# A list scheduler is replaced by one written-out order of all operations

## The chip, the cores and the metric

The kernel runs on one core of one Trainium2 chip. The metric is the device time of one execution in microseconds (us). Inputs and outputs are bf16.

## The reference

Two layers are computed on the same weights, each an attention block and a gated feed-forward block (FFN), for 2048 tokens of 512 features. The attention has 32 heads of 16 features and works on 4 segments of 512 tokens: inside a segment it is causal softmax attention, and a memory matrix `M` and a vector `z` carry the earlier segments.

```python
for s in range(N):                       # N = 4 segments of L = 512 tokens
    logits = einsum('bhqd,bhkd->bhqk', qs, ks) * scale + mask
    a_dot = softmax(logits) @ vs
    pq = phi(qs)                         # t + 1 where t > 0, else exp(t)
    a_mem = (pq @ M) / (pq @ z + 1e-06)
    o = g * a_mem + (1 - g) * a_dot      # g = sigmoid(beta)
    M, z = M + phi(ks).T @ vs, z + sum(phi(ks))
...
x = x + A(layernorm(x)); x = x + B(layernorm(x))   # B: (silu(x@w1) * (x@w3)) @ w2
x = x + A(layernorm(x)); x = x + B(layernorm(x))   # the second layer, same weights
```

## The kernel before

The work is cut into eight stages, numbered 0 to 7: four segments of layer one, then four of layer two. `build` adds 3629 operations to a `Sched` object, stage by stage. An operation is one instruction or a small fixed group of them (a score block is eight matmuls or four), with what it reads and writes and the engines that may run it. `add` numbers them in the order in which they are added (`seq`). Names that the text uses, written name/stage:

- `xt`, `xT`: normalised x turned over, on TensorE or by a DMA transpose on SP's queue; `q`, `k`, `v`: projections, four matmuls to a tile; `evq`, `evk`, `evv`, `evX`: copies of a PSUM bank to SBUF, which ScalarE or VectorE may run (`ev`).
- `R0.0` to `R0.19`: the score blocks of a stage (`attention`; stage 0 is done in two halves and has 40). Each fills all of the PSUM space for scores (two slots `S` of two banks), and one `exp` on ScalarE empties it, so a score block waits for the exp of the one before. GpSimd then cuts the causal corner (`mask`, an affine_select).
- `C0.0` to `C3.0`: exp times values; then `evX`, a DMA transpose `XT`, the division (`rd`, `rdg`, `t2`, `oadd` on VectorE or GpSimd), a DMA transpose `oT`, and the output projection `o0` to `o3`.
- `phexp`, `ph1`, `phmin`: phi; `dacc`, `mden`, `mnum`: the memory's update and reading; `lnve`, `lnrs`, `norm`, `bnst`, `bnag`: layer norm.
- `r`, `g`, `u`, `d`: the FFN's matmuls, eleven to a tile for `d`, four for `g` and `u`; `tanh`, `gp`, `hm`: its gating on ScalarE and VectorE.

PSUM is cut into two slots `S` for scores and four banks `B` that all other matmuls share. TensorE has three ways of working: whole array (F), four row groups (R, the score blocks), four column groups (C, the products with values). `shape` looks at what stands between two score blocks: where a C operation is among them and all others can be cut, these are issued as four quarter matmuls (`quarters`, L393) instead of one whole (`whole`, L388).

The order on each engine comes from `schedule`, a list scheduler: it keeps modelled times, offers each engine its ready operations and takes one by priority, margins and look-ahead (`PRIO`, `GATE`, `FINE`, `MARGIN`, `SLACK`, `LOOK`). The order is fixed when the program is built; on the chip each engine runs its list from front to back, and waits on semaphores where an operand, a buffer or a bank isn't ready. `hand_over` then adds dependencies that the data doesn't need: an instruction of GpSimd waits for the VectorE instructions of certain kinds (`SHARED`) that stand ahead of it, if its modelled start is less than 2 us behind theirs. `finalize` turns dependencies into waits.

Of the kernel before, what the change touches and what calls it, by code (L numbers as in the profile page):

```python
# [9 lines left out]
T = 2048  # L10
# [15 lines left out]
DMA_K = 8  # L26
LAT = 80.0
LAT_SAME = 30.0
DMA_SLACK = 1200.0
LOAD_RATE = 280.0  # L30
PE_SWITCH = 100.0
PE_TAIL = 170.0
R_SLACK = 0.0
SLACK = {"pe": 37.0, "act": 72.0, "dve": 89.0, "pool": 112.0, "sp": 27.0}
LOOK = {"pe": 91.0, "act": 30.0, "dve": 20.0, "pool": 80.0, "sp": 302.0}
C_AGE = 6933.0
MARGIN = {"": 50.0, "XT": 1200.0, "bnag": 500.0, "bnst": 100.0, "d": 200.0, "dacc": 300.0, "evX": 100.0, "evk": 500.0, "evq": 100.0, "evv": 300.0, "exp": 50.0, "g": 50.0, "gpr": 200.0, "hT": 100.0, "hmr": 500.0, "k": 50.0, "ldbeta": 500.0, "ldw": 500.0, "ldwk": 50.0, "ldwo": 3000.0, "ldwq": 300.0, "ldwv": 800.0, "ldx": 50.0, "lnrs": 800.0, "lnve": 300.0, "macc": 50.0, "mask": 50.0, "mblk": 500.0, "mde": 200.0, "mden": 200.0, "mnum": 500.0, "mrec": 1200.0, "norm": 300.0, "oT": 3000.0, "oadd": 500.0, "om": 50.0, "ph": 500.0, "phexp": 200.0, "phmin": 300.0, "pkT": 3000.0, "q": 200.0, "r": 300.0, "resA": 100.0, "resB": 500.0, "stx": 300.0, "t": 2000.0, "tanh": 50.0, "u": 50.0, "warm": 100.0, "xT": 800.0, "xt": 200.0}
# [23 lines left out]
class Op:  # L61
    __slots__ = ("opts", "eng", "fn", "dmaq", "deps", "gates", "prio", "mode", "bufs", "nblock", "succ", "seq",
                 "issued", "start", "end", "lane", "val", "vc", "waits", "name", "size", "avail_at", "hold", "group", "wide", "flex")


class Sched:
# [16 lines left out]
    def add(self, opts, fn, reads=(), writes=(), bufs=(), prio=0.0, mode=None, dmaq=None, name="", gates=(), size=0,  # L83
            hold=(), after=(), flex=False):

        op = Op()
        op.opts = {e: (o, l) for e, o, l in opts}
        op.fn, op.dmaq, op.prio, op.mode, op.name, op.size = fn, dmaq, prio, mode, name, size
        op.bufs = tuple(bufs)
        op.hold = tuple(hold)  # L90
        op.issued = False
        op.avail_at = 0.0
        op.end = 1e12
        op.eng = None
        op.wide = None
# [3 lines left out]
        deps = {}  # L99
# [17 lines left out]
        op.gates = [g for g in gates if g is not None]  # L117
# [6 lines left out]
    @staticmethod  # L124
    def _lat(d, e):
        if d.dmaq is not None:
            return LAT + (DMA_SLACK if e in ("pe", "dve") else 0.0)
        return LAT_SAME if d.eng == e else LAT

    def settle(self, unit_ops, prio, gate, fine):  # L130

        order = list(unit_ops)
        place = {u: i for i, u in enumerate(order)}
        seen = {}
        for op in self.ops:
            key = (op.name, op.group[1])
            seen[key] = seen.get(key, -1) + 1
            op.prio += prio.get(op.group, 0.0) + fine.get(key + (seen[key],), 0.0)
            out = []
            for x in op.gates:  # L140
                if not isinstance(x, tuple):
                    out.append(x)
                elif x in place:
                    i = place[x] + gate.get(op.group, 0)
                    if i >= 0:
                        out.append(unit_ops[order[min(i, len(order) - 1)]])
            op.gates = out

    def schedule(self):
        avail = {e: [] for e in ENGS}  # L150
        for op in self.ops:
            op.succ = []
            op.nblock = 0
        for op in self.ops:
            for d in list(op.deps.values()) + op.gates:
                d.succ.append(op)
                op.nblock += 1
        for op in self.ops:
            if op.nblock == 0:
                for e in op.opts:  # L160
                    avail[e].append(op)
        t_free = {e: 0.0 for e in ENGS}
        busy = {e: 0.0 for e in ENGS}
        dma_free = 0.0
        xpose_free = {}
        pe_mode = "F"
        dma_count = {}
        dma_hist = {}
        order = {e: [] for e in ENGS}
        issue = []  # L170
        left = len(self.ops)
        count = {e: 0 for e in ENGS}
        while left:
            best = None
            for e in ENGS:
                tf = t_free[e]
                cands = []
                smin = None
                for op in avail[e]:
                    s = op.avail_at if op.gates else 0.0  # L180
                    for d in op.deps.values():
                        if e == "pe" and d.eng == "pe" and d.dmaq is None:
                            continue
                        r = d.end + self._lat(d, e)
                        if r > s:
                            s = r
                    ok = True
                    for b in op.bufs:
                        if b.slot is None:
                            if not b.pool.free:  # L190
                                ok = False
                                break
                            r = min(self._slot_ready(b.pool, i, e) for i in b.pool.free)
                        else:
                            r = self._prev_ready(b.prev, e)
                        if r > s:
                            s = r
                    need = {}
                    for b in op.hold + op.bufs:
                        if b.slot is None:  # L200
                            need[b.pool.name] = need.get(b.pool.name, 0) + 1
                            if need[b.pool.name] > len(b.pool.free):
                                ok = False
                    if not ok:
                        continue
                    w = max(tf, s + (R_SLACK if op.mode == "R" else SLACK[e]) + MARGIN.get(op.group[0], 0.0))
                    s = max(tf, s)
                    cands.append((s, w, op))
                    if smin is None or w < smin:
                        smin = w  # L210
                if not cands:
                    continue
                lim = max(smin, tf) + LOOK[e]
                pick = None
                for s, w, op in cands:
                    if w > lim:
                        continue
                    pr = op.prio
                    if e == "pe" and op.mode == "C":
                        if pe_mode == "F" and s - op.avail_at < C_AGE:  # L220
                            pr = 1e5 + pr
                        else:
                            pr = -1e5 + pr
                    if pick is None or (pr, s, op.seq) < pick[0]:
                        pick = ((pr, s, op.seq), s, op)
                s, op = pick[1], pick[2]
                if best is None or s < best[0]:
                    best = (s, e, op)
            if best is None:
                raise RuntimeError("stuck: " + "; ".join(  # L230
                    "%s %s" % (op.name, [b.pool.name for b in op.bufs + op.hold if b.slot is None]) for e in ENGS for op in avail[e][:4]))
            s, e, op = best
            if e == "pe" and op.mode != pe_mode:
                s += PE_SWITCH
                pe_mode = op.mode
            for x in op.opts:
                avail[x].remove(op)
            op.eng = e
            op.issued = True
            op.start = s  # L240
            occ, lat = op.opts[e]
            for b in op.hold + op.bufs:
                if b.slot is None:
                    i = min(b.pool.free, key=lambda i: (self._slot_ready(b.pool, i, e), i))
                    b.pool.free.remove(i)
                    b.slot = i
                    b.prev = b.pool.prev[i]
            for b in op.bufs:
                for d in b.prev:
                    if d is not op:  # L250
                        op.deps[d.seq] = d
                b.left -= 1
                if b.left == 0:
                    b.pool.free.append(b.slot)
                    b.pool.prev[b.slot] = b.users
            if op.dmaq is None:
                op.end = s + lat
                t_free[e] = s + occ
                count[e] += 1
                op.lane = self._lane(("eng", e))  # L260
                op.val = count[e]
            else:
                if op.mode == "T":
# [3 lines left out]
                    if dma_free > x0:  # L267
                        dma_free += 500.0
# [958 lines left out]
```

## Time and profile before

| | |
|---|---|
| time, median of 3 runs | 481.24 us (481.15 to 481.86) |
| span of the profiled execution | 480.1 us |
| what lies around the span, median less span | 1.2 us |
| TensorE busy | 470.7 us, 98% of the span |
| ScalarE, VectorE, GpSimd busy | 390.3, 388.1, 242.6 us |

The span is that of the profiled execution, from its first instruction to its last. Matmuls are pipelined and their ends are modelled: two of them that follow each other overlap in the rows, so the busy time of TensorE counts as busy some time in which it could have begun another matmul.

### The profile page before, as it was taken

Reading aid. Unit: us, or ns where it says so; the run is one execution under the profiler, and the core shown is the slowest. Engines: PE = TensorE matmul, PEld = TensorE weight load, DVE = VectorE, ACT = ScalarE, POOL = GpSimd, SP = SyncE. Lnnn points to the kernel's source line nnn. Section 1 sums busy time; section 2 is a strip of 40 time slices with the busy share of each in tenths; the row PEclk is TensorE's granted clock in tenths of the full one; section 3 lists DMA queues with packets and bytes.
Section 4 is the critical chain, followed back from the end, with each engine's and each line's share of the span. In section 5 each row is a group of like instructions: output and inputs, shape, how many; then the busy total and the mean of one; then the engine's idle time right before and its main releaser. Section 6 shows DMA issues by size and latency. Waiting matters only on the chain.

```text
span 480.1 us, 14316 instructions
## 1 busy us (share of the span) xinstructions
PE 470.7 (98%) x6122; PEld 221.4 (46%) x6122; DVE 388.1 (81%) x816; ACT 390.3 (81%) x351; POOL 242.6 (51%) x383
## 2 busy tenths in 40 slices
PE   8999999999999999999999999999999999999997
PEld 4443446754444344434444444544444344454544
DVE  6988889896988879979987699785985696478672
ACT  3999999988899898899989999889889898930220
POOL 4867484854477545555555355445567456530000
PEclk9999999999999999999999999999999999999999
DMA  8794654423156421471552425431137224320301
GB/s 258 269 155 96 102 123 89 66 52 69 23 89 100 68 35 32 80 110 25 84 84 56 78 46 108 60 59 29 35 45 114 64 29 83 67 47 25 90 3 45
DMA packets 106527, 37.15 MB, mean 77 GB/s; under 512 B 99200, under 2 KB 104448, under 8 KB 106464
## 3 DMA queue, kind: packets, MB, share of 16 engines
q1 hardware_dynamic: 104016, 31.41, 34.7%
q0 software_dynamic: 1488, 4.03, 3.9%
q8 instruction: 48, 0.79, 0.7%
q10 hardware_dynamic: 960, 0.79, 0.5%
q14 instruction: 15, 0.12, 0.1%
HBM read 8.43 MB, written 2.10 MB: 22 GB/s over the span
## 4 chain that ended last, share of the span: by engine, by line
PE 79%; ACT 12%; DMA 3%; DVE 3%; POOL 1%; issue 0%; ACTq 0%; POOLq 0%; DVEq 0%
PE psall L388 45%; PE psall L393 19%; ACT e L958 10%; PE psall L949 9%; PE psall L1000 6%; ACT px L807 1%; DMA xg<-xs 1%; DMA x_tok<-in_A_x_dram 1%; DMA W<-og 1%; DMA W<-xn 1%; POOL e L971 1%; PE psall L834 0%; POOL og L1033 0%; DVE ln L687 0%; DVE W L811 0%
## 5 line engine op out<-in xcount | busy, mean ns | idle before, releaser
L958 ACT ACTIVATE e<-psall 128x2048 bf16<-128x2048 f32 (+1 forms) x180 | 301.5, 1722 | 31.8 <-PE psall L949 30.6
L971 POOL TENSOR_SCALAR_AFFINE_SELECT e<-e 128x512 bf16<-128x512 bf16 x256 | 160.8, 646 | 166.0 <-ACT e L958 115.4
L388 PE MATMUL psall<-W,w 128*128 128x512 bf16 (+1 forms) x494 | 103.4, 351 | 0.5 <-DVE W L546 0.3
L388 PEld LDWEIGHTS psall<-W,w 128*128 128x128 bf16 x494 | 44.8, 98 | 43.5 <-issue 7.7
L1117 DVE SCALAR_TENSOR_TENSOR gp<-th,psall 128x512 bf16<-128x512 bf16 x80 | 53.6, 678 | 12.2 <-ACT th L1115 11.6
L1115 ACT ACTIVATE th<-psall 128x512 bf16<-128x512 f32 x80 | 47.1, 600 | 18.2 <-PE psall L393 17.3
L1121 DVE SCALAR_TENSOR_TENSOR h<-gp,psall 128x512 bf16<-128x512 bf16 x80 | 53.9, 680 | 9.8 <-PE psall L388 8.7
L388 PE MATMUL psall<-w,h 128*128 128x512 bf16 (+1 forms) x216 | 51.9, 380 | 0.0
L393 PE MATMUL psall<-W,w 128*32 128x512 bf16 (+1 forms) x904 | 49.9, 368 | 0.0
L687 DVE BATCH_NORM_STATS2 ln<-x_tok 128x6 f32<-128x512 bf16 x64 | 42.4, 678 | 1.5 <-DMA x_tok<-in_A_x_dram 1.2
L949 PE MATMUL psall<-W 16*128 16x256 bf16 (+3 forms) x544 | 41.7, 294 | 1.0 <-ACT e L958 1.0
L1000 PE MATMUL psall<-e,va 128*32 128x256 bf16 (+3 forms) x1088 | 41.4, 293 | 0.4 <-POOL e L971 0.3
L949 PE MATMUL psall<-W,km 32*128 32x256 bf16 (+3 forms) x544 | 41.1, 291 | 0.4 <-ACT e L958 0.2
L1140 DVE TENSOR_TENSOR x_tok<-psall,x_tok 128x512 bf16<-128x512 f32 (+1 forms) x33 | 22.0, 668 | 21.4 <-PE psall L388 12.3
L546 DVE CAST W<-psall 128x512 bf16<-128x512 f32 x46 | 31.2, 681 | 5.5 <-PE psall L388 5.5
L546 DVE CAST xs<-psall 128x512 bf16<-128x512 f32 x38 | 25.6, 680 | 11.4 <-PE psall L1000 11.3
L949 PEld LDWEIGHTS psall<-W 16*128 16x128 bf16 x544 | 13.2, 91 | 44.9 <-ACT e L958 41.1
L1000 PEld LDWEIGHTS psall<-e,va 128*32 128x32 bf16 x1088 | 24.2, 96 | 18.7 <-POOL e L971 3.1
L393 PEld LDWEIGHTS psall<-W,w 128*32 128x32 bf16 x904 | 23.2, 97 | 20.5 <-issue 0.9
L388 PE MATMUL psall<-W,wk 128*128 128x512 bf16 (+1 forms) x131 | 31.9, 354 | 0.7 <-DVE W L546 0.5
L393 PE MATMUL psall<-w,h 128*32 128x512 bf16 (+3 forms) x588 | 32.0, 363 | 0.0
L1033 POOL TENSOR_TENSOR og<-xg,rd 128x256 bf16<-128x256 bf16 (+1 forms) x46 | 26.0, 581 | 10.4 <-DVE rd L1027 7.3
(85 smaller groups left out, 591.8 us busy)
## 6 DMA issues: line engine op xcount, KB each, us to landing
w<-in_B_w_dram SPq DMA_DIRECT2D x4, 688.0 KB, 8.5
out_dram<-x_tok SPq DMA_DIRECT2D x15, 128.0 KB, 1.7
km<-W POOLq DMA_DIRECT2D x24, 64.0 KB, 2.9
w<-in_B_w_dram POOLq DMA_DIRECT2D x3, 384.0 KB, 3.7
x_tok<-in_A_x_dram POOLq DMA_DIRECT2D x2, 512.0 KB, 4.9
xg<-xs SPq DMA_TRANSPOSE x36, 3.2
W<-og SPq DMA_TRANSPOSE x36, 2.5
wk<-in_A_wk_dram SPq DMA_DIRECT2D x1, 512.0 KB, 4.8
```

The source lines that it names most:

```text
L388: return e.matmul(out, lhsT, rhs, **k)
L393: o = e.matmul(out[c:c + 32], lhsT[:, c:c + 32], rhs, tile_position=(0, c), **k)
L546: return e.tensor_copy(dst(), src())
L687: dve(lambda e: e.bn_stats(ln_r[st.slot][:, i, 0:6], x_tok[:, tt, :]), 540, reads=[("x", tt)], writes=[(st, 0, i)], bufs=[st], prio=prio, ...
L949: o = e.matmul(S4[:, sps(pg), c:c + n], kk[32 * pg:32 * pg + r, G, 128 * j:128 * j + 128], q_r[z.q.slot][32 * pg:32 * pg + r, G, 128 * t1 ...
L958: act(lambda e, N=N, ebuf=ebuf, pgs=pgs, sps=sps: e.activation(e_r[ebuf.slot][:, pgs[0]:pgs[-1] + 1, 0:N], S4[:, sps(pgs[0]):sps(pgs[-1]) ...
L971: pool(lambda e, ebuf=ebuf, c=c: e.affine_select(e_r[ebuf.slot][:, :, c:c + 128], e_r[ebuf.slot][:, :, c:c + 128], pattern=[[0, 4], [1, 128]],
L1000: o = e.matmul(bank(X)[32 * pg:32 * pg + 32, base + W - n:base + W], va_r[z.va.slot][:, j, h:h + 32], e_r[eb.slot][:, pg, c:c + n], start= ...
L1033: return e.tensor_tensor(ogv()[:, 0:nt, :, k, :], src, v(1)[:, k, :, :, None].to_broadcast([P, nt, 4, DH]), ALU.mult)
L1115: act(lambda e, NW=NW, B=B, th=th: e.activation(th_r[th.slot][:, 0:NW], bank(B)[:, 0:NW], ACT.Tanh, scale=0.5), NW, reads=[(B, 0)], writes ...
L1117: dve(lambda e, NW=NW, B=B, th=th, gp=gp: e.scalar_tensor_tensor(gp_r[gp.slot][:, 0:NW], th_r[th.slot][:, 0:NW], 1.0, bank(B)[:, 0:NW], AL ...
L1121: dve(lambda e, NW=NW, B=B, gp=gps[fg], h=hs[fg]: e.scalar_tensor_tensor(h_r[h.slot][:, 0:NW], gp_r[gp.slot][:, 0:NW], 0.5, bank(B)[:, 0:N ...
```

## The change

`schedule` no longer schedules. It reads the order of all 3629 operations from a list of their numbers (`ORDER`), and takes the second of an operation's two possible engines for the 188 numbers in `OTHER`. The list is one for all engines; each engine takes its own out of it in that order. Buffer slots are handed out first in, first out. All priorities, margins, gates and cost parameters are gone. In place of `hand_over` each GpSimd instruction that isn't a DMA waits for all `SHARED` operations of VectorE that stand between it and the GpSimd instruction ahead of it, however far back they are.

```diff
     def schedule(self):
-        avail = {e: [] for e in ENGS}
...
+        self.issue = []
+        for run in ORDER.split():
+            a, _, b = run.partition("-")
+            self.issue += self.ops[int(a):int(b or a) + 1]
+        other = {int(x) for x in OTHER.split()}
+        self.order = {e: [] for e in ENGS}
...
+        for place, op in enumerate(self.issue):
+            e = op.eng = op.opts[1 if op.seq in other else 0]
+            op.place = place
             for b in op.hold + op.bufs:
                 if b.slot is None:
-                    i = min(b.pool.free, key=lambda i: (self._slot_ready(b.pool, i, e), i))
...
+                    b.slot = b.pool.free.pop(0)
+                    b.prev = b.pool.prev[b.slot]
...
+            if e == "dve" and op.group[0] in SHARED:
+                handed.append(op)
+            elif e == "pool" and op.dmaq is None:
+                for d in handed:
+                    op.deps[d.seq] = d
+                handed = []
+            self.order[e].append(op)
...
-    def hand_over(self):
-
-        place = {op.seq: n for n, op in enumerate(self.issue)}
-        todo = [op for op in self.order["pool"] if op.dmaq is None]
-        for d in self.order["dve"]:
-            if d.group[0] not in SHARED or d.start > HAND_OVER:
-                continue
-            while todo and place[todo[0].seq] < place[d.seq]:
-                todo.pop(0)
-            if todo and todo[0].start < d.start + 2000.0:
-                todo[0].deps[d.seq] = d
...
-            need = sorted((d for d in bylane.values() if kn[d.lane] < d.val), key=lambda d: -d.end)
+            need = sorted((d for d in bylane.values() if kn[d.lane] < d.val), key=lambda d: -d.place)
...
+ORDER = """
+    24 8 1 23 26 25 28 27 29 4 0 16 9 2 5 3 18 10 6-7 11 17 19 12 22 20-21 32 13-14 30 15 33 31 34 42 35 55 54 36
...
+    1124 1102-1105 770 747 774 771 1289 333-335 1162 1125 336 375 374 748 1290 743 1293 1116 744 784 776 785 1137
+    1117-1118 377 1136 378-380 382-385 775 1291 381 386 376 772 745 769 788 746 1119 869 396 870 1120 387 1138 397
...
+    1223-1224 643 1593 1590 644 1539-1542 628-630 1226 1543 910 631-632 1227 1533 633 645 1230 1594 1208 1210 1240
...
+    1000-1004 1969 1264 1970-1971 1950 1612 1951 1972 1282 1611 1958 1610 2114 1613 1959 2115-2116 1615 1614
+    1960-1961 1987-1990 1616 1982-1983 1962 1952 1617 1984-1985 989-992 1992 1619 1993-1994 993 1991 1995 1986 1266
...
+    3421 3410 3422 3416 3423-3424 3411 3425 3185-3190 3141-3144 3191 3426 3431 3427 3433 3429 3428 3434 3432 3430
+    3435 3192 3145 3136-3140 3172-3182 3159-3169 3436-3439 3441 3440 3442 3193-3194 3183 3195-3197 3184 3146-3154
+    3443 3155-3156 3444 3448 3157-3158 3449-3450 3445 3170 3446-3447 3451-3452 3454-3457 3460-3463 3453 3488-3489
...
-    S.settle(units, PRIO, GATE, FINE)
```

What the numbers in these lines are: 377 to 380 are `o2`/0, 382 to 385 `o3`/0, 770, 784 and 788 the score blocks `R0.6`, `R0.7`, `R0.8` of stage 1; 1226 and 1240 are `R0.11` and `R0.12` of stage 2, 631 and 632 two matmuls of `d2`/0, 1230 `C1.0`/2, 1594 `mden`/3; 1612 and 1616 are `R0.2` and `R0.3` of stage 3, 1951, 1958 to 1961 and 1987 to 1990 the nine matmuls between them, 2114 a `phexp`, 1613 the exp behind it; 3425 is the last matmul of `o3`/7, 3185 to 3195 are `d3`/6, 3172 to 3182 `d2`/6, 3159 to 3169 `d1`/6, 3146 to 3156 `d0`/6, 3141 to 3144 `u9`/6, 3136 to 3139 `u8`/6, 3443, 3444 and 3448 `r0`, `r1` and `r2` of stage 7, whose input two `xT` transposes bring (3439 and 3442).

## Rows read from the trace of the kernel before

**Rows 1.** The page's first part: busy time, share of the span, instructions of each engine.
```profile
span 480.1 us, 14316 instructions
...
PE 470.7 (98%) x6122; PEld 221.4 (46%) x6122; DVE 388.1 (81%) x816; ACT 390.3 (81%) x351; POOL 242.6 (51%) x383
```

**Rows 2.** Busy us by stretch: its length, PE, PEld, DVE, ACT, POOL, clock, DMA.
```profile
0.00:11.00 11.00, 8.75 (x62) 4.79 (x64) 6.97 (x21) 3.07 (x4) 5.82 (x17) 1.00 0.78 246
11.00:62.00 51.00, 50.60 (x722) 22.41 (x711) 45.79 (x113) 50.75 (x56) 33.02 (x54) 1.00 0.69 159
62.00:118.00 56.00, 54.22 (x860) 32.50 (x861) 48.17 (x104) 52.30 (x47) 34.01 (x53) 1.00 0.44 79
118.00:420.00 302.00, 300.89 (x3372) 132.51 (x3374) 248.66 (x510) 272.15 (x226) 164.57 (x253) 1.00 0.38 64
420.00:449.00 29.00, 28.67 (x564) 14.38 (x560) 21.35 (x41) 5.69 (x11) 5.14 (x7) 1.00 0.25 57
449.00:477.00 28.00, 27.58 (x572) 14.86 (x572) 17.14 (x29) 6.30 (x11) 0.00 (x0) 1.00 0.09 26
```

**Rows 3.** TensorE's timeline around seven holes: start, us, instruction, idle before, its releaser.
```profile
69.60 0.83 PE L393 MATMUL psall<-wo,W 128*32 128x512 bf16 x12 [0.60 <-DMA W<-og]
...
76.42 0.83 PE L388 MATMUL psall<-W,w 128*128 128x256 bf16 x6 [0.35 <-DVE W L546]
...
81.35 0.40 PE L949 MATMUL psall<-W 16*128 16x512 bf16 x4 [0.26 <-ACT e L958]
...
86.24 0.29 PE L949 MATMUL psall<-W 16*128 16x256 bf16 x4 [0.18 <-ACT e L958]
...
137.58 0.29 PE L949 MATMUL psall<-W 16*128 16x256 bf16 x4 [0.55 <-ACT e L958]
...
157.52 0.82 PE L388 MATMUL psall<-W,wk 128*128 128x512 bf16 x3 [0.22 <-DVE gp L1117]
...
438.81 9.04 PE L393 MATMUL psall<-w,h 128*32 128x512 bf16 x164
...
448.93 0.27 PE L393 MATMUL psall<-w,W 128*32 128x192 bf16 x4 [0.33 <-DMA W<-xn]
```

**Rows 4.** TensorE's timeline, one run of whole matmuls between two score blocks.
```profile
218.30 0.39 PE L949 MATMUL psall<-W,km 32*128 32x512 bf16 x4
...
219.28 1.89 PE L388 MATMUL psall<-wv,W 128*128 128x512 bf16 x8
221.10 0.40 PE L949 MATMUL psall<-W,km 32*128 32x384 bf16 x8
```

**Rows 5.** ScalarE's timeline over the same run.
```profile
217.93 1.05 ACT L807 ACTIVATE px<-W 128x1024 bf16<-128x1024 bf16 x1
218.87 1.87 ACT L958 ACTIVATE e<-psall 128x2048 bf16<-128x2048 f32 x1
```

**Rows 6.** ScalarE's groups by form: busy us, mean ns, idle before and its releasers.
```profile
L958 ACT ACTIVATE e<-psall 128x2048 bf16<-128x2048 f32 x140 | 263.6, 1883 | 31.1 <-PE psall L949 30.0
...
L807 ACT ACTIVATE px<-W 128x1024 bf16<-128x1024 bf16 x24 | 26.7, 1111 | 0.3 <-DVE W L546 0.2
L545 ACT ACTIVATE xs<-psall 128x512 bf16<-128x512 f32 x26 | 15.8, 608 | 1.5 <-PE psall L1000 1.5
```

**Rows 7.** Waits, engine and line, for whom: us in total, times, longest.
```profile
POOL e L971 <- ACT e L958: 115.4, 90, 3.7
...
POOL e L971 <- DVE xn L705: 14.2, 14, 2.4
...
PEld psall L1000 <- POOL e L971: 3.1, 8, 0.7
```

**Rows 8.** A VectorE line by itself: duration ns min/median/max.
```profile
L705 DVE TENSOR_SCALAR xn<-x_tok,ln x64: 318/406/787, 6.2 to 444.7; 128x512 bf16<-128x512 bf16 x64
```

**Rows 9.** Another VectorE line, with a PSUM operand: duration ns min/median/max.
```profile
L1121 DVE SCALAR_TENSOR_TENSOR h<-gp,psall x80: 620/681/689, 81.2 to 467.2; 128x512 bf16<-128x512 bf16 x80
```

**Rows 10.** Waits of SP's DMA queue: us in total, times, longest.
```profile
SPq L1041 <- POOL e L971: 48.8, 14, 10.0
```

More of the change, by code (lines that the diff above doesn't have):

```diff
@@ L26 @@
 DMA_K = 8
[L27 to L31, printed above, removed]
-PE_TAIL = 170.0
[L33 to L37, printed above, removed]
+PE_TAIL = 170.0
 class Pool:
@@ L61 @@
 class Op:
-    __slots__ = ("opts", "eng", "fn", "dmaq", "deps", "gates", "prio", "mode", "bufs", "nblock", "succ", "seq",
-                 "issued", "start", "end", "lane", "val", "vc", "waits", "name", "size", "avail_at", "hold", "group", "wide", "flex")
+    __slots__ = ("opts", "eng", "fn", "dmaq", "deps", "mode", "bufs", "hold", "seq", "place", "lane", "val", "vc", "waits", "name",
+                 "group", "wide", "flex", "gates")
 class Sched:
@@ L86, in add @@
         op = Op()
-        op.opts = {e: (o, l) for e, o, l in opts}
-        op.fn, op.dmaq, op.prio, op.mode, op.name, op.size = fn, dmaq, prio, mode, name, size
+        op.opts = [e for e, _, _ in opts]
+        op.fn, op.dmaq, op.mode, op.name = fn, dmaq, mode, name
         op.bufs = tuple(bufs)
         op.hold = tuple(hold)
-        op.issued = False
-        op.avail_at = 0.0
-        op.end = 1e12
         op.eng = None
+        op.gates = []
         op.wide = None
@@ L116, in add @@
         op.deps = deps
-        op.gates = [g for g in gates if g is not None]
         for b in op.bufs:
@@ L122, in add @@
         return op
[L124 to L147, printed above, removed]
@@ L149, in schedule @@
-    def schedule(self):
-        avail = {e: [] for e in ENGS}
[L151 to L171, printed above, removed]
-        count = {e: 0 for e in ENGS}
[L173 to L182, printed above, removed]
-                            continue
[L184 to L241, printed above, removed]
@@ new lines, in schedule @@
+    def schedule(self):
+        self.issue = []
[4 more added lines that the diff above has]
+        self.order = {e: [] for e in ENGS}
+        count = {e: 0 for e in ENGS}
+        sent = {}
+        handed = []
+        for place, op in enumerate(self.issue):
+            e = op.eng = op.opts[1 if op.seq in other else 0]
+            op.place = place
@@ L284, in schedule @@
-            busy[e] += occ
-            order[e].append(op)
-            issue.append(op)
-            left -= 1
-            for nx in op.succ:
-                nx.nblock -= 1
-                if nx.nblock == 0:
-                    nx.avail_at = s
-                    for x in nx.opts:
-                        avail[x].append(nx)
-        self.order, self.issue, self.busy = order, issue, busy
-        self.hand_over()
+                op.lane, op.val = self._lane(("eng", e)), count[e]
+            else:
+                q = sent.setdefault(op.dmaq, [])
+                n = len(q)
+                op.lane, op.val = self._lane(("dma", op.dmaq, n % DMA_K)), 16 * (n // DMA_K + 1)
+                if n >= DMA_K:
+                    op.deps[q[n - DMA_K].seq] = q[n - DMA_K]
+                q.append(op)
@@ L296, in schedule @@
+            if e == "dve" and op.group[0] in SHARED:
[3 more added lines that the diff above has]
+                    op.deps[d.seq] = d
+                handed = []
+            self.order[e].append(op)
+        assert sorted(op.seq for op in self.issue) == list(range(len(self.ops)))
+        for op in self.issue:
+            assert all(d.place < op.place for d in op.deps.values())
         self.shape()
-        self.t_total = max(op.end for op in self.ops)
@@ L397 @@
 SHARED = ("norm", "lnve", "t", "rdg", "ph", "phmin", "mblk", "km", "oadd")
-HAND_OVER = 1e9
 def o_act(n, psum=True):
@@ L454, in build @@
+"""
+OTHER = """
[8 rows of a table added]
+"""
 def build(nc, A_x, A_wq, A_wk, A_wv, A_wo, A_beta, B_w1, B_w3, B_w2, out):
```

180 lines of the change are left out of this document (121 added, 59 removed), and 19 rows, old and new, of tables (FINE, OTHER).

## The prediction

> **What bounds the kernel now.** The page comes first: TensorE is busy for 470.7 of 480.1 us, ScalarE and VectorE for 81% each [rows 1]. So the order can only win what TensorE idles, and the next view is where it does. By stretches [rows 2] it idles 2.25 us in the first 11 us (loads and the first layer norm), 0.40 from 11 to 62, 1.78 from 62 to 118, 1.11 from 118 to 420, 0.33 from 420 to 449 and 0.42 behind that; about 3 us more lie behind its last matmul. Between 11 and 449 us that is 3.62 us, and the change is mostly about them.
>
> The timeline shows them as separate holes. Seven stand in [rows 3], with 2.49 of the 3.62 us; the reader is to see that they have different releasers: a DMA transpose twice, ScalarE's exp three times, VectorE twice. A hole is longer than the idle time shown. Eight whole matmuls fill 1.89 us and each is drawn 0.38 us long [rows 4], so one begins every (1.89 - 0.38) / 7 = 0.216 us, and each is drawn 0.16 us past the point where the next could begin. I add 0.16 us to each hole.
>
> The last view is the beat of the attention. A score block waits for the exp ahead of it. A run of eleven matmuls lasts 2.80 us from score block to score block (218.30 to 221.10) [rows 4], of which 11 x 0.216 = 2.38 are the matmuls and 0.42 the score block and two changes of mode. So a run of n matmuls lasts 0.42 + 0.216 n: nine make 2.37 us. ScalarE needs 1.88 for the exp and whatever stands ahead of it: 1.11 for a `phexp`, 0.61 for a bank copy [rows 6]. TensorE is the bound by a little; where the order gives ScalarE too much in one run, or TensorE too little, a hole appears.
>
> **The change part by part.** *The same work.* The list holds the same 3629 operations. Counted from both orders, TensorE changes its mode 357 times in place of 358, and 497 operations are cut into quarters in place of 490. A change of mode is about 0.1 us (eight matmuls from 219.28 would let the next begin at 221.01, the score block begins at 221.10 [rows 4]), and a quartered operation streams as fast as a whole one: 164 quarters, 41 operations, take 9.04 us, 0.22 each [rows 3]. Together: -0.1 us.
>
> *Four holes that the list fills.* At 69.60, `o2`/0 waits for the transpose of `og`; it stood ahead of score block `R0.6`. Now it stands behind `R0.7` (784, then 377), one run and two score blocks later, at least 2.4 us by the beat, against a hole of 0.60. At 137.58 the run ahead of `R0.12` of stage 2 held `C1.0` and one `mnum`, too little for the exp; now it holds two matmuls of `d2`/0, `C1.0` and `mden`, so the two alone add 0.43 and the rest at least nothing, against 0.55. At 448.93, `r2`/7 waits for the transpose of the layer norm; between the last `o`/7 and the `r`s stood 41 operations [rows 3]. In the new list 50 stand ahead of `r0`, and two more ahead of `r2`: 11 x 0.216 = 2.4 us more cover, against 0.33. At 86.24 the run of stage 1 that held `C1.0`, `dacc` and three `u` now holds eight `u` ahead of `C1.0` and three behind it, half-size matmuls of about 0.11: +0.9 less `dacc`, against 0.18. Sum: 0.60 + 0.55 + 0.33 + 0.18 + 4 x 0.16 = 2.3 us. What moves into these runs leaves others; it is late there only if that run falls under the exp's need, which is the part after next.
>
> *The other holes.* The three left in [rows 3] (0.35, 0.26, 0.22) and those not shown (3.62 - 2.49 = 1.13) make 1.96 us, with 0.16 for each of the three 2.4. The list rewrites their surroundings (1026 of 1931 neighbouring pairs on TensorE stay), but I see no single move that closes them. Ends: 0 and 2.4; I take half, 1.2, since nothing in the rows favours either end.
>
> *New pressure on ScalarE.* Six bank copies leave it (0.61 each, 3.6 us of 390). But the list puts short runs beside long ScalarE work. Between `R0.2` and `R0.3` of stage 3 (1612 to 1616) stand nine matmuls, 2.37 us, and a `phexp` with an exp, 1.11 + 1.88 = 2.99: short by 0.62. Counted like this over stages 2 to 7, eleven runs fall short by more than 0.45 us, 6.5 us together (the longest 0.79); the old order had two such. A shortage isn't all lost. In [rows 4, 5] eleven matmuls, 2.80, stand against the same 2.99, short by 0.19, yet there is no hole: the `phexp` began 0.37 us ahead of the score block, and the exp ended at 220.74, 0.36 us ahead of the next. So ScalarE may be short by 0.19 + 0.36 = 0.55 when it comes early. By that row the eleven cost 0.7 us in all; if ScalarE isn't early, 6.5. I take 1.1, near the end that a row shows.
>
> *VectorE and its queue.* It gains six copies at about 0.68 (as [rows 9], also with a PSUM operand) and loses one `t2`: 388.1 becomes about 392 of 480. What hides this is TensorE's runs; without cover each copy holds one of the four banks 0.68 us longer, as the holes of 76.42 and 157.52 show (0.35 and 0.22). Nothing is added for it.
>
> *The hand-over to GpSimd.* Counted from both orders, 215 VectorE operations are handed over in place of 191, to 97 GpSimd instructions in place of 131. A wait there holds the masks queued behind it, and those hold a C operation. GpSimd is busy for half the span [rows 1], already waits 14.2 us for `norm` alone, and TensorE waits for masks 3.1 us [rows 7]. Ends: -3.1 and +3.1; I take 0, since the masks mostly wait for the exp (115.4 us) and their consumers stand two score blocks later.
>
> The trace shows the reason for such waits: `norm`, with all operands in SBUF, takes from 318 to 787 ns with a median of 406 [rows 8], while an instruction with a PSUM operand stays between 620 and 689 [rows 9]. The Trainium skill (GPSIMD Engine Reference, section 1, Specifications) says that GpSimd shares its SBUF interfaces with VectorE, with contention when VectorE runs in a 2-port mode or with two SBUF inputs; the spread agrees, though no row here isolates it. By that rule VectorE would come earlier wherever the new waits keep the two apart, which is the first rival below; by the rows alone the term stays 0.
>
> *SP's queue, start and end.* The transposes on SP go in a new order, and its queue stands behind waits for masks for 48.8 us [rows 10]; a transpose in the wrong place would make a hole like the one at 69.60, 0.8 us. I take 0, with one such as bound. The first score block still has the same projections ahead of it, and the last piece is still half a tile of `d3`: 0.
>
> **The sum.** -0.1 - 2.3 - 1.2 + 1.1 = -2.5 us. The profiled execution: span 480.1, to 477.6; with the 1.2 us that lie around it, against the median of 481.24, **478.7 us**.
>
> **The rivals.**
> 1. *All holes close.* VectorE comes earlier because the port is free, the 2.4 us of other holes go wholly, and ScalarE's shortage costs nothing: -0.1 - 2.3 - 2.4 = -4.8, 476.4 us. For it: two of the holes end with VectorE. Against it: one list for all engines can't please every run.
> 2. *No change.* TensorE's work is the same, and each hole closed is paid by another of its size, since work moved into one run leaves another: 481.2 us. For it: TensorE is at 98%. Against it: three of the four closed holes are late data, which a move cures without cost.
> 3. *ScalarE becomes the bound in the attention* (the other side). At the eleven short runs it isn't early, so each costs its full shortage: -3.6 + 6.5 = +2.9, 484.1 us. It decides from 3.6 us on, a third of a microsecond for each. For it: several come close to each other, so that one exp's delay passes to the next; [rows 5] has only one. Against it: six copies less on ScalarE.
>
> **How the numbers follow.** Forecast (476.8 to 480.2 us, from just above rival 1 to a gain that can just be told) 0.55; rival 1 (below 476.8), 0.13; rival 2, 0.14; rival 3 and, in part, a transpose issued late, 0.18. A measurement of this kernel tells about 0.2%, 0.96 us, from no change. Faster by more: 0.55 + 0.13 = 0.68; within: 0.14; slower: 0.18. The range of 475.4 to 482.9 leaves out 0.07 below (the hand-over's gain on top of rival 1) and 0.12 above, most of rival 3.
>
> **What would show it.** Right: idle of TensorE from 11 to 449 us falls from 3.62 to about 2, the holes at `o2`/0, ahead of `R0.12` of stage 2 and at `r2`/7 are gone, and those left end with ScalarE. Rival 3 would show as holes of 0.3 us and more ahead of score blocks in stages 2 to 6, with an exp as their releaser; rival 1 as less than 1 us idle and a median of `norm` near its 318 ns. Wrong: a C operation that waits for GpSimd in every stage, or an `o` or `r` behind a transpose that SP issued late.

## The result: slower by 0.6%, and the profile after

The kernel after takes 484.34 us (median, 483.28 to 485.49), before beside it 481.19 us: ratio 1.0061, 95% interval 1.0044 to 1.0079. Forecast were 478.7 us and a range of 475.4 to 482.9. The profiled execution has a span of 482.4 us, 2.3 more than before's [rows 1]. Two slow runs of `b_shift56` (492.7 and 492.8 us, at a granted clock of 0.976) are left out of its time and ratio further down.

The page of the kernel after, its busy times and the shares of the chain that ended last:

```profile
span 482.4 us, 14409 instructions
...
PE 469.9 (97%) x6197; PEld 225.2 (47%) x6197; DVE 390.5 (81%) x821; ACT 389.2 (81%) x345; POOL 245.7 (51%) x384
...
PE 89%; DVE 6%; DMA 3%; issue 1%; POOL 0%; DVEq 0%; ACT 0%
```

The work is the same. ScalarE has no share in the chain, and none of the holes shown below ends with an exp: rival 3 didn't happen. Where TensorE idles, by the stretches of [rows 2]:

```profile
11.00:62.00 51.00, 51.00 (x690) 23.41 (x684) 47.80 (x112) 50.86 (x51) 31.71 (x53) 1.00 0.58 138
62.00:118.00 56.00, 51.53 (x914) 31.64 (x913) 47.74 (x103) 49.48 (x43) 32.43 (x51) 1.00 0.52 96
118.00:420.00 302.00, 300.21 (x3393) 133.54 (x3389) 245.80 (x509) 273.87 (x227) 168.35 (x256) 1.00 0.33 61
420.00:449.00 29.00, 28.27 (x536) 13.92 (x529) 22.70 (x46) 5.72 (x10) 7.39 (x9) 1.00 0.41 57
```

From 11 to 449 us it is 6.99 us instead of 3.62, where I forecast 2. From 11 to 62 nothing is left; most of the growth lies between 62 and 118 us (4.47 instead of 1.78). TensorE's timeline around the eight longest holes, columns as in [rows 3]:

```profile
72.16 0.81 PE L226 MATMUL psall<-wo,W 128*128 128x512 bf16 x3 [1.87 <-DVE W L759]
...
84.52 0.67 PE L948 MATMUL psall<-e,va 128*32 128x512 bf16 x12 [0.69 <-POOL e L919]
...
90.52 0.71 PE L226 MATMUL psall<-W,w 128*128 128x256 bf16 x5 [1.34 <-DMA W<-xn]
...
109.37 0.94 PE L948 MATMUL psall<-e,va 128*32 128x512 bf16 x20 [0.27 <-DVE x_tok L1088]
...
223.88 0.48 PE L226 MATMUL psall<-mb,W 128*128 128x8 bf16 x12 [0.49 <-DVE W L759]
...
262.09 0.61 PE L226 MATMUL psall<-W,w 128*128 128x512 bf16 x2 [1.27 <-DVE macc L789]
...
430.74 0.61 PE L231 MATMUL psall<-W,w 128*32 128x512 bf16 x8 [0.52 <-DVE h L1069]
...
436.74 1.05 PE L231 MATMUL psall<-wo,W 128*32 128x512 bf16 x16 [0.21 <-DVE gp L1065]
```

Many small holes became a few long ones, with releasers of three kinds (VectorE, GpSimd, a DMA transpose). Two labels hide the cause. At 72.16 stands `o2`/0, which reads the transpose of `og` issued at 67.82 and landed at 72.07 (4.2 us); the VectorE line named had been done before. The chain that leads to this transpose begins with `rd`/0 in VectorE's timeline:

```profile
64.64 0.24 DVE L973 RECIPROCAL rd<-xg 128x16 f32<-128x16 bf16 x1
...
65.69 0.17 DVE L975 TENSOR_TENSOR rd<-rd,gg 128x16 f32<-128x16 f32 x1
```

and goes on over GpSimd to SP's queue:

```profile
66.99 0.80 POOL L981 TENSOR_TENSOR og<-xg,rd 128x128 bf16<-128x128 bf16 x2
...
67.82 1.93 SPq L989 DMA_TRANSPOSE W<-og  x1
```

At 262.09 stands `g3`/3, whose bank `macc`/5 frees on VectorE, and VectorE's timeline shows what held that:

```profile
258.45 0.35 DVE L1040 SCALAR_TENSOR_TENSOR hr<-gp,psall 128x192 bf16<-128x192 bf16 x1
260.66 0.36 DVE L973 RECIPROCAL rd<-xg 128x32 f32<-128x32 bf16 x1 [1.85 <-DMA xg<-xs]
261.05 0.19 DVE L975 TENSOR_TENSOR rd<-rd,gg 128x32 f32<-128x32 f32 x1
261.16 0.73 DVE L653 TENSOR_SCALAR xn<-x_tok,ln 128x512 bf16<-128x512 bf16 x2
261.81 0.22 DVE L789 TENSOR_TENSOR macc<-psall,macc 128x68 f32<-128x68 f32 x1
```

`rd`/4 waits 1.85 us for a transpose of `xs`, and `macc`/5, whose data were there at 259.52, waits behind it. The hole at 430.74 is the same with `rd`/7 and `hm`/6. At 90.52 a transpose of `xn` is late itself. Four of the eight thus stand behind a transpose.

To add holes up I use one measure: the start of a matmul, less that of the one ahead, less the time of that one's columns at 2.4 GHz (once for four quarters), less the usual cost of the change of mode. The sum over the kernel is 13.74 us before and 16.00 after: +2.26, the difference of the spans.

### The profile page after: what moved, and what is told of

The parts are those of the page before. It is cut to its first block, busy times and chain, and to the rows that moved or that the text cites. A ratio compares the mean times of both kernels' runs of the same rounds, so it can differ in the third digit from the quotient of the medians.

```text
span 482.4 us, 14409 instructions
## 1 busy us (share of the span) xinstructions
PE 469.9 (97%) x6197; PEld 225.2 (47%) x6197; DVE 390.5 (81%) x821; ACT 389.2 (81%) x345; POOL 245.7 (51%) x384
## 4 chain that ended last, share of the span: by engine, by line
PE 89%; DVE 6%; DMA 3%; issue 1%; POOL 0%; DVEq 0%; ACT 0%
PE psall L226 50%; PE psall L231 19%; PE psall L897 11%; PE psall L948 7%; DMA xg<-xs 2%; PE psall L524 1%; DMA W<-xn 1%; DVE xn L653 1%; DVE W L759 1%; DVE h L1069 1%; DVE W L494 1%; PE psall L782 1%; DVE gp L1065 1%; DVE ln L635 0%; PE psall L665 0%
## 5 line engine op out<-in xcount | busy, mean ns | idle before, releaser
L226 PE MATMUL psall<-W,w 128*128 128x512 bf16 (+1 forms) x458 | 101.2, 354 | 2.6 <-DMA W<-xn 1.3
L226 PEld LDWEIGHTS psall<-W,w 128*128 128x128 bf16 x458 | 41.1, 98 | 44.5 <-issue 7.2
L231 PE MATMUL psall<-W,w 128*32 128x512 bf16 (+1 forms) x1048 | 56.6, 360 | 0.5 <-DVE h L1069 0.5
L226 PE MATMUL psall<-w,h 128*128 128x512 bf16 (+1 forms) x220 | 56.9, 380 | 0.0
L494 DVE CAST W<-psall 128x512 bf16<-128x512 f32 x51 | 34.3, 682 | 6.3 <-PE psall L226 5.5
L231 PEld LDWEIGHTS psall<-W,w 128*32 128x32 bf16 x1048 | 27.6, 97 | 22.5 <-issue 1.7
L948 PEld LDWEIGHTS psall<-e,va 128*32 128x32 bf16 x1088 | 26.1, 97 | 18.3 <-issue 2.3
L494 DVE CAST xs<-psall 128x512 bf16<-128x512 f32 x44 | 29.5, 681 | 5.4 <-PE psall L948 5.4
L226 PE MATMUL psall<-wv,W 128*128 128x512 bf16 x122 | 33.5, 380 | 0.0
L231 PE MATMUL psall<-w,h 128*32 128x512 bf16 (+2 forms) x572 | 32.4, 364 | 0.0
```

Source lines behind the costliest of these rows:

```text
L226: return e.matmul(out, lhsT, rhs, **k)
L231: o = e.matmul(out[c:c + 32], lhsT[:, c:c + 32], rhs, tile_position=(0, c), **k)
L494: return e.tensor_copy(dst(), src())
L948: o = e.matmul(bank(X)[32 * pg:32 * pg + 32, base + W - n:base + W], va_r[z.va.slot][:, j, h:h + 32], e_r[eb.slot][:, pg, c:c + n], start= ...
```

## The experiments

Two theories stood after the result. **H**: the hand-over holds GpSimd. **F**: transposes land late since TensorE's own instruction fetch runs beside them, and the new order leaves them too little cover (time between a transpose's issue and its first reader). F came from the packets: TensorE's instructions come in packets of 16 KB, 49 in this run, one for about 253 of its 12394 matmuls and weight loads. A fetch counts here as in flight beside a transpose when it begins between 0.2 us ahead of the transpose's issue and its landing. In the kernel after 25 of 32 transposes with such a fetch in flight landed over 0.7 us later than the median of their kind, and 4 of 89 without one.

**The order or the scheduler around it.** `b_list` writes the old order and choice of engines out as a list for the new scheduler.

```diff
 ORDER = """
-    (the order of after)
+    (the 3629 operations as the kernel before issues them)
```

> The kernel before's order of every engine and its choice of engines, written out as a list and put out by the scheduler of after (its rules for slots and its hand-over: 216 edges instead of 191). Theory 'order': it runs as before, 481.2 within 0.5. Theory 'machinery' (what the new scheduler puts around any order costs, not the order): 483 to 484.5.

481.46 us, ratio to before 1.0002 (0.9991 to 1.0012). The rules for slots, and 25 hand-over edges more, cost nothing that can be seen; the loss comes with the new order. Whether the order itself makes it, this run doesn't say.

**The hand-over.** `a_nohand` drops all its edges, `a_oneedge` those of one mask.

```diff
             elif e == "pool" and op.dmaq is None:
                 for d in handed:
-                    op.deps[d.seq] = d
+                    if op.seq != 793:            # a_oneedge; a_nohand drops the loop
+                        op.deps[d.seq] = d
                 handed = []
```

> The kernel after, without the hand-over edges: GpSimd waits for a VectorE operation only where it needs its data. Everything else, every engine's order too, as after. Theory H (the hand-over is what costs: it holds GpSimd 28.1 us after against 14.0 before, the longest one 4.3 us at 75 to 79.8 us with masks, lnrs/0 and norm/0 queued behind it): the holes at 84.5 (0.86 us) and 90.5 (1.51) shrink or go, some smaller ones too, and the time falls 2 to 3 us, to about 481.5. Theory F (DMA transposes that land 1 to 1.5 us late since TensorE's instruction fetch is in flight beside them, with too little cover in the new order): only the hole at 84.5 goes, the holes at 72.2, 262 and 431 stay within 0.3 us, and the time falls at most 0.9, to about 483.5. A third outcome is a loss: VectorE's big operations get longer by more than the waits saved (phmin 675 ns clear against 899 overlapped in the run of after), 485 to 487.

> The kernel after, with one GpSimd instruction alone, the mask at 75 us that waits for lnve/0, freed of its hand-over edges. Theory H with this one edge as its core: masks and lnrs/0 start 3 to 4 us earlier, norm/0 and xT/0 too, the holes at 84.5 and 90.5 go, and the time falls 2.2 us, to 482.1. Theory F: the hole at 84.5 goes (0.86), the hole at 90.5 stays or moves with the next fetch, time 483.5. If neither: within 0.3 of after.

`a_nohand`: 492.5 us, ratio 1.0242 (1.0221 to 1.0264), 8.2 us above after: the third outcome, and larger. VectorE's busy time rises from 390.5 to 400.8 us. Its `norm` line by itself (duration ns min/median/max), first in after, then in `a_nohand`:

```profile
L653 DVE TENSOR_SCALAR xn<-x_tok,ln x64: 396/407/1312, 6.1 to 444.8; 128x512 bf16<-128x512 bf16 x64
```

```profile
L651 DVE TENSOR_SCALAR xn<-x_tok,ln x64: 399/409/3068, 6.5 to 453.5; 128x512 bf16<-128x512 bf16 x64
```

The 3068 ns are the third of the `norm`s in this row of `a_nohand`'s VectorE timeline (it begins at 148.10):

```profile
147.32 3.85 DVE L651 TENSOR_SCALAR xn<-x_tok,ln 128x512 bf16<-128x512 bf16 x3
```

and this is GpSimd's beside it:

```profile
147.98 3.04 POOL L917 TENSOR_SCALAR_AFFINE_SELECT e<-e 128x512 bf16<-128x512 bf16 x5
```

The `norm` began 0.12 us after five masks in a row had begun and ended 0.15 us after the last of them; `hm` and a bank waited behind it, and TensorE stood for 2.43 us at 151.82. The Trainium skill (SBUF — State Buffer, "SBUF: two separate sides") says that the pair of ports that GpSimd shares with certain VectorE instructions (those in a 2-port mode, or with two inputs in SBUF) is a lock, held for a whole instruction by whoever starts first. The trace agrees, and shows more: the loser sat out five instructions. Not all of the 8.2 us is such waiting: behind two holes TensorE's granted clock fell to 0.50 (last section), which by the windows there costs some 3.4 us.

`a_oneedge`: 482.59 us, ratio to before 1.0035 (1.0016 to 1.0054), 1.75 us under after. GpSimd's timeline in after, where the edge stands:

```profile
73.95 1.58 POOL L484 DMA_DIRECT2D w<-in_B_w_dram  x2
79.81 2.84 POOL L919 TENSOR_SCALAR_AFFINE_SELECT e<-e 128x512 bf16<-128x512 bf16 x4 [4.27 <-DVE ln L641]
82.62 1.15 POOL L644 TENSOR_TENSOR ln<-ln,mhalf 128x2 f32<-128x2 f32 x1
83.74 1.22 POOL L919 TENSOR_SCALAR_AFFINE_SELECT e<-e 128x512 bf16<-128x512 bf16 x2
```

and in `a_oneedge`:

```profile
79.22 2.92 POOL L920 TENSOR_SCALAR_AFFINE_SELECT e<-e 128x512 bf16<-128x512 bf16 x4 [3.50 <-ACT e L907]
82.11 0.71 POOL L645 TENSOR_TENSOR ln<-ln,mhalf 128x2 f32<-128x2 f32 x1
82.80 1.26 POOL L920 TENSOR_SCALAR_AFFINE_SELECT e<-e 128x512 bf16<-128x512 bf16 x2
```

The masks and `lnrs`/0 come only 0.5 to 0.9 us earlier, since an exp ends the wait instead; I had expected 3 to 4. That is enough for the hole at 84.5. The next one stays, as F says, since a fetch is in flight beside its transpose again (4.9 us):

```profile
90.11 1.14 PE L227 MATMUL psall<-W,w 128*128 128x256 bf16 x9 [1.62 <-DMA W<-xn]
```

The rest of the gain is the hole at 262, which is gone though nothing near it was changed: its transpose landed after 3.2 us (at 258.41), only 0.19 us behind the begin of the next fetch. The two holes together were 2.3 us, so some 0.5 us came back in other places.

**Moving the fetches alone.** The warm-up matmuls at the start are cut into shorter ones, columns unchanged; nothing reads their result. 84 more instructions stand in TensorE's queue, so each later fetch falls about 84 instructions earlier in the work.

```diff
-            for _ in range(2):
-                o = e.matmul(bank(B), xs_r[0][:, 0, 0:128], xs_r[0][:, 0, :], start=True, stop=True)
+            for c in range(0, 1024, 128):
+                o = e.matmul(bank(B)[:, c % 512:c % 512 + 128], xs_r[0][:, 0, 0:128],
+                             xs_r[0][:, 0, c % 512:c % 512 + 128], start=True, stop=True)
```

> The kernel after, with the warm-up's 14 matmuls of 512 columns cut into 56 of 128 columns: the same columns, 84 more instructions in TensorE's queue (matmuls and weight loads), whose result nothing reads. It moves the places at which TensorE's queue asks for its next instructions, and nothing else. Theory F: other transposes are hit; at least three of the four holes behind late transposes (72.2: 2.04 us, 90.5: 1.51, 262: 1.43, 431: 0.69) change by over 0.5 us, new ones of that kind may come, and the time moves by 0.7 us or more either way. Theory H: holes and time stay within 0.4 us of after (484.3), warm-up aside.

479.64 us, ratio to before 0.9962 (0.9948 to 0.9975): 4.7 us under after, and faster than before. All four holes change by more than 0.5 us, as F has it and H hasn't: 2.04 to 0.68, and 1.51, 1.43 and 0.69 to nothing. Why is seen in the packets around the transpose of `xs` that held `rd`/4. In after (from its issue to its landing; the DMA row is the busy share of the 16 engines in 40 slices of 0.13 us):

```profile
DMA  9960000007999999996489999900000000000010
...
q8 instruction: 1, 0.02, 1.2%
issues: line engine op xcount, KB each, median us to landing
xg<-xs SPq DMA_TRANSPOSE x1, 5.2
```

and in `a_shift84` around the same transpose (slices of 0.08 us):

```profile
DMA  0299999500000017999999999999995459999995
...
q1 hardware_dynamic: 2074, 0.51, 80.1%
issues: line engine op xcount, KB each, median us to landing
xg<-xs SPq DMA_TRANSPOSE x1, 3.2
```

In after the fetch starts at 258.73, in slice 26 of the 40; directly after it the engines are all but idle for 1.6 us, and only then the transpose lands. In `a_shift84` no instruction packet is in the window, and it lands after 3.2 us. Over the 18 traces that could be read whole, 392 of 621 transposes with a fetch of TensorE's in flight are late (63%), 92 of 1495 without (6%). The medians of the five kinds are 0.9 to 1.2 us longer with one. A transpose that is late has more time to meet a fetch, so a count is needed that doesn't depend on its length: where a fetch began 1 to 2 us behind the issue, 144 of 147 are late; where it began 1 to 2 us ahead of it, 25 of 286.

The other cuts of the warm-up are written like this, with 3, 5, 6, 7 or 8 pieces for each matmul:

```diff
+            for c, d in [(i * 512 // 6, (i + 1) * 512 // 6) for _ in range(2) for i in range(6)]:
+                o = e.matmul(bank(B)[:, c:d], xs_r[0][:, 0, 0:128], xs_r[0][:, 0, c:d], start=True, stop=True)
```

> The kernel after, the warm-up's 14 matmuls cut into 84 pieces: 140 more instructions in TensorE's queue, columns as before; the result of these matmuls is not read. Theory F, that late transposes are those with one of TensorE's instruction fetches beside them: the fetches fall at yet other places (140 of the 256 instructions that a 16 KB fetch would hold at 64 bytes each, against 84 in the first shift), other transposes are late, and the time differs from both 484.3 and 479.6 by 0.7 us or more, between 478.5 and 485.5. If the gain of the first shift came from shorter warm-up pieces and not from the place of the fetches, it gives 479.6 again within 0.4.

> The kernel after, the warm-up cut into 112 pieces: 196 more instructions in TensorE's queue; the result is not read. Theory F: as the last, between 478.5 and 485.5, with its own set of late transposes, each with a fetch in flight. Rival: 479.6 again within 0.4.

> The kernel before with the first shift (84 more instructions in TensorE's queue, result not read). If the order of before has more time between a transpose and its reader, its time stays within 0.6 us of 481.5 at every place of the fetches, and the new order's loss is one of cover. If before's order is hit as much as after's, it moves by 1 us or more.

> The kernel before with 196 more instructions in TensorE's queue (result not read). As for the shift by 84: within 0.6 us of 481.5 if its order has cover, 1 us or more off if the time of before was itself a matter of where the fetches fell.

> The kernel before with 140 more instructions in TensorE's queue (result not read): the fourth place of the fetches for it. Before gave 481.5, 482.7 and 485.1 at the other three, after 484.3, 479.6 and 487.2 there, and 483.6 here. Between 480.5 and 485; the mean of the four places then says which order is faster whatever the fetches do: after's is 483.7.

> The kernel after, warm-up cut into 42 pieces: 56 more instructions in TensorE's queue (result not read). If the miss is where the fetches fall: anywhere from 479.5 to 487, and the mean of after over all places within 0.7 of before's. If the new order is slower by itself: 483.5 or more here and at 112 and 168, and its mean 1 us or more above before's.

> The kernel before with the same cut (result not read): 481.3 to 485.1 as at its other places.

> The kernel after with 112 more instructions in TensorE's queue (result not read): as for 56; anywhere from 479.5 to 487 by the fetches, 483.5 or more if the order is slower by itself.

> The kernel before with 112 more instructions in TensorE's queue (result not read): 481.3 to 485.1.

> The kernel after with 168 more instructions in TensorE's queue (result not read). If neighbouring places of the fetches hit the same transposes: between its neighbours, 483.6 and 487.2. If each place is its own draw: 479.5 to 487.

> The kernel before with 168 more instructions in TensorE's queue (result not read): between its neighbours, 482.2 and 485.1, or 481.3 to 485.1 if each place is its own draw.

What they gave, the ratios to before as it stands, with 95% intervals:

| more instructions | after's order, us | ratio | before's order, us | ratio |
|---|---|---|---|---|
| 0 | 484.34 | 1.0061 (1.0044 to 1.0079) | 481.19 | 1 |
| 56 | 480.76 | 0.9986 (0.9975 to 0.9998) | 482.24 | 1.0017 (0.9993 to 1.0041) |
| 84 | 479.64 | 0.9962 (0.9948 to 0.9975) | 482.74 | 1.0034 (1.0008 to 1.0061) |
| 112 | 482.16 | 1.0018 (1.0002 to 1.0033) | 481.89 | 1.0008 (0.9993 to 1.0023) |
| 140 | 483.59 | 1.0034 (1.0016 to 1.0051) | 482.25 | 1.0014 (1.0002 to 1.0025) |
| 168 | 482.35 | 1.0022 (1.0004 to 1.0040) | 484.78 | 1.0072 (1.0049 to 1.0094) |
| 196 | 487.24 | 1.0115 (1.0083 to 1.0148) | 485.08 | 1.0061 (1.0039 to 1.0082) |
| mean | | 1.0028 | | 1.0029 |

`a_shift196` lies outside the range given for it (487.24 against 485.5); the others stayed in theirs, and before's order is hit too (84 and 196 moved it by more than 1 us). Shorter warm-up pieces by themselves give nothing (140 and 196 are slow); each place is its own draw (168 isn't between its neighbours for after's order), and the sign between the orders goes either way. The mean difference is -0.01%, with a standard error of 0.19% from its seven values, so a 95% interval of about 0.47%, 2.3 us, either way: by itself the new order is neither faster nor slower, as far as seven places can tell. The forecast gain of 2.5 us lies just outside that interval; a gain or loss of 1 or 2 us isn't excluded. It spreads more, 1.5% against 0.7%.

**Giving the late transposes room.** `a_moves` moves three groups of the list (332 to 336: `rd`, `rdg`, two `t2` and the `oT` of the hole at 72.2, earlier; `rd`/4 behind `macc`/5; `rd`/7 and its `t2` behind `hm`/6).

```diff
-... 739-740 1153 370 1154 368 322 1157 ... 332 369 ... 1289 333-335 1162 1125 336 375
+... 739-740 332-335 1153 370 1154 368 322 336 1157 ... 369 ... 1289 1162 1125 375
-... 2775 2086-2087 2777 2554 2098 1787 2776 1768 2077 2555 1774-1775
+... 2775 2777 2554 2098 1787 2776 1768 2077 2555 2086-2087 1774-1775
-... 3101-3102 3068-3069 3401-3402 3404 3403 3115-3118
+... 3101-3102 3068-3069 3115-3118 3401-3402 3404 3403
```

> The kernel after with three places of its list changed, so that fewer things stand behind a transpose on VectorE: rd/0 and rdg/0 of the last chunk (64.6 us) go before two bnst, and t2/0 and oT/0 with them; rd/4 (260.7) goes behind macc/5; rd/7 and its t2 (428.7) go behind hm/6. If the loss is late transposes with too little cover: the holes at 72.2 (2.04 us), 262 (1.43) and 431 (0.69) shrink by 1.2 or more, 1.2 and 0.5, and the time falls by 2 to 3.5 us, to between 480.8 and 482.3, less what fetches that fall on other transposes cost (1 us either way). If the holes come back behind other instructions of VectorE: within 0.7 of 484.3.

> The last kernel and the one hand-over edge freed as well. The edge's own hole (84.5, 0.86 us) goes: 0.9 to 1.8 us under the last kernel, 479.5 to 481.4.

> The last kernel and the first shift of TensorE's fetches (84 more instructions in its warm-up, whose result is not read). The shift alone gave 479.6; of its holes the moves take the one at 70.9 (0.68 us) and the edge the one at 83.3 (0.2): 478.5 to 479.2, under both kernels, if the fetches stay where the shift put them. If the moves shift transposes under other fetches: up to 481.

`a_moves`: 482.32 us, ratio 1.0018 (1.0007 to 1.0028), 2.0 under after, at the upper end (482.3) of what was expected. The holes at 72.2, 262 and 431 are gone, which would be 4 us; TensorE's timeline shows where half of it went:

```profile
74.44 0.76 PE L231 MATMUL psall<-w,W 128*32 128x192 bf16 x28 [0.67 <-DMA W<-xn]
...
89.50 1.25 PE L226 MATMUL psall<-W,w 128*128 128x256 bf16 x10 [1.61 <-DMA W<-xn]
...
433.06 1.05 PE L231 MATMUL psall<-wo,W 128*32 128x512 bf16 x16 [1.32 <-DMA W<-og]
```

All three wait for a transpose that a fetch was beside; the second stood in after too (1.34 at 90.52), the other two are new. `a_moves_edge`: 482.17 us, ratio 1.0015 (1.0005 to 1.0025), no more than `a_moves`, where the stall ahead of the `C` operation of the edge had already shrunk from 0.86 to 0.21 us; my 0.9 to 1.8 was wrong. `a_moves_edge_84`: 479.87 us, ratio 0.9970 (0.9959 to 0.9981), the same as `a_shift84` alone: the hole at 70.9 went, and the next, behind a transpose of `xn` that takes 6.1 us, grew from 0.69 to 0.97. Both beat the two kernels, but by a place of the fetches found by trial, for exactly this stream of instructions; at that place the moves gain nothing, and that they gain at all rests on the one place without a shift.

## Why the prediction was wrong

The failed step, the one that put the time outside the range, is that on SP's queue: "I take 0, with one such as bound", one hole of 0.8 us. I looked at when a transpose is issued, not at how long it takes, and took its 2.5 or 3.2 us (the medians of the kinds) as fixed. With a fetch of TensorE's beside them the medians are about 1 us longer, and the one shown took 5.2 us instead of 3.2. To tell this from the order I took each operation's stall at six places of the fetches (the traces at 168 lack matmul records) and its median over them as the order's own. Those medians add up to 12.46 us for before's order and 12.29 for after's: -0.17. At the places of the two kernels as they stand, the stalls over and under their medians add 2.96 - 1.68 = +1.28 before and 4.11 - 0.40 = +3.71 after: +2.43. Together +2.26, the loss between the two traces. Three of after's four holes behind transposes (90.5, 262, 431) have medians of 0.12, 0 and 0.07; they are draws, not the order. A second step failed beside it, and on the mean over the places it takes the forecast gain away: the new stalls in the list below, most of which stand behind VectorE's queue, which the sum had at 0.

The other steps, by the same medians:

- **What bounds the kernel.** Right, but two of the holes in [rows 3] weren't the order's: `o2`/0 at 69.60, 0.79 us, is 0 to 0.11 at the five other places of before's order, and the one at 157.52, 0.38 us, is 0 at all five (ahead of it a transpose of `xs` took 5.63 us, from 150.91, with a fetch beside it).
- **Four holes, -2.3.** Three closed: `R0.12`/2 from 0.62 to 0, `r2`/7 from 0.50 to 0, `R0.12`/1 from 0.27 to 0.01, 1.4 us where I had 1.54. The fourth grew to 2.0 us: `o2`/0 went 2.4 us later as I counted, but VectorE's list put `rd`/0 at 64.64, 7 us behind its data (57.63), so the `oT` behind it was issued at 67.82. I moved the reader and didn't follow the chain that feeds it. That chain alone costs 0.68 us: at the two places where no fetch met this `oT` (56 and 84) it landed after 2.9 us, and that is the hole; at the four others it took 4.1 to 5.4 us and the hole was 2 us and more.
- **Other holes, -1.2.** Too little: stalls that shrink by 0.1 us or more add up to 5.05 us, 3.7 without those three.
- **ScalarE, +1.1.** Too much: no score block of stages 2 to 6 gains a stall of 0.1 us, the largest is +0.18 at `R0.6`/1.
- **VectorE's queue, "nothing is added".** Wrong by 1.3: `mden`/5 +0.56 (behind `phmin`), `o1`/7 +0.38 (a bank, behind `gp`), `C3.0`/1 +0.32 (a bank, behind `resB`), each there at nearly all places.
- **Hand-over, 0.** +0.85 at `C1.0`/1, inside the bounds of 3.1; as a whole it is worth 8.2 us at the one place measured, far more than I had seen in the spread of [rows 8].
- **Rival 2** was held unlikely since "three of the four closed holes are late data". By [rows 3] two are (69.60 and 448.93); the other two end with an exp.
- Mode changes, start and end: no difference that can be seen beside these.

So the gain was there and larger than forecast, and some 5 us of new stalls, five operations with 4.1 of them (1.3 of these need a fetch at `o2`/0), took it back: that is rival 2, no change, and the means over seven places agree with it within their 2.3 us. The measured loss on top of it is where the fetches fell. The forecast had no term for that, so a time nearer to it at another place (479.64 at 84) would have been luck. That a fetch, and not something that comes with it, halts the transposes rests on the shifts and the packets; a kernel in which one single fetch is moved was not tried. What makes the 6% late without a fetch stays open; they are mostly the same transposes in one trace after the other (in after's order the two of `xs` at 191.9 and 193.2, in 19 of the 20 cases without a fetch), so that part goes with the order and not with the fetches.

## What to carry to other kernels

A hole behind a DMA transpose in one trace may be a draw: before pricing it, shift the instruction stream by some 50 to 200 instructions that nothing reads and see which holes stay. When an order is compared with another by half a per cent, compare them over several such shifts. When a reader is moved later, follow the chain that feeds it through every in-order queue, and put whatever waits for a transpose on VectorE behind what frees banks.

## What the runs showed of the hardware that was not expected

- A 16 KB instruction fetch of TensorE's, on a queue of its own (q8), is followed in the window shown by about 1.6 us in which the transposes in flight make next to no progress (5.2 us instead of 3.2).
- A VectorE instruction with its operands in SBUF can sit out five GpSimd masks in a row: 3068 ns instead of 409.
- A hole can cost more than its length. In `a_shift140` TensorE stands for 3.06 us ahead of 73.67 (in after 1.87 there), and within that hole its granted clock falls to 0.50, the lower level of 1.2 GHz, and stays there behind it; the windows of that run:

```profile
70.50:73.60 3.10, 0.11 (x1) 0.00 (x0) 1.44 (x3) 2.78 (x3) 1.59 (x3) 0.82 0.83 77
73.60:76.00 2.40, 2.33 (x6) 0.89 (x7) 0.43 (x1) 0.00 (x0) 2.26 (x4) 0.50 1.03 186
76.00:78.00 2.00, 2.00 (x11) 0.78 (x9) 0.98 (x3) 0.00 (x0) 0.00 (x0) 0.50 0.82 297
78.00:80.00 2.00, 2.00 (x84) 1.59 (x84) 1.46 (x4) 1.74 (x1) 0.00 (x0) 0.68 1.06 199
```

From 73.6 to 80 that is 2.4 x 0.50 + 2 x 0.50 + 2 x 0.32 = 2.8 us of full clock lost, nearly as much as the hole; in after, with 1.87 us, the clock there stays at 1.00. `a_nohand` shows the same behind two holes:

```profile
73.50:77.00 3.50, 3.48 (x16) 1.53 (x16) 1.10 (x2) 1.04 (x2) 2.16 (x3) 0.59 0.95 174
77.00:80.00 3.00, 3.00 (x116) 2.10 (x116) 2.57 (x6) 2.34 (x3) 0.00 (x0) 0.91 1.06 261
...
151.80:156.00 4.20, 4.18 (x28) 1.25 (x32) 2.77 (x5) 1.32 (x2) 0.00 (x0) 0.60 0.65 125
```

That is 3.5 x 0.41 + 3 x 0.09 + 4.2 x 0.40 = 3.4 us. The length of a hole alone doesn't tell whether the clock falls: the first of these two was 1.65 us, shorter than the 1.87 of after, where it didn't. And a place of the fetches isn't one time: of the ten runs of `a_shift140` the two with a mean granted clock of 1.000 took 481.5 and 481.8 us, the eight with 0.992 to 0.996 took 482.8 to 484.5.
